# Pooled attention and a two-layer FFN on one core: the products with v in two rows of five and four key tiles per half of the queries instead of three rows of three, and p in a ring of tiles by key tile

## The chip, the cores and the metric

The kernel runs on one core of one Trainium2 chip. The metric is the device time of one launch in microseconds (us). TensorE (PE) multiplies, VectorE (DVE), ScalarE (ACT) and GpSimd (POOL) work elementwise, SyncE (SP) issues the DMAs. ns are nanoseconds.

## The reference

For 8 batches and 8 heads there are 1152 positions of 64 numbers. Pairs of neighbouring queries are averaged, so 576 queries attend to 1152 keys; the heads' results are put side by side to 4608 tokens of 512 numbers, which go through an FFN with 2048 hidden numbers.

```python
q_pool = q.reshape(B, H, S // factor, factor, D).mean(axis=3)
scores = scale * np.matmul(q_pool, k.transpose(0, 1, 3, 2))
scores = scores - np.max(scores, axis=-1, keepdims=True)
attn = np.exp(scores)
attn = attn / (np.sum(attn, axis=-1, keepdims=True) + 1e-09)
return np.matmul(attn, v).astype(np.float32)
...
h = x @ w_in
g = h - np.tanh(h)
return (g @ w_out).astype(np.float32)
```

## The kernel before

**Two stages.** The attention stage runs to about 995 us. It writes the unnormalized products with v to `x_dram` and the sums of the exponentials to `z_dram`. The FFN stage loads x back by chunks of tokens, multiplies it by the reciprocals of the sums (POOL, lines 118 to 120) and runs two layers of matmuls (`hidden`, line 521, and `second`, line 546).

**Pairs and units.** Attention goes over 32 pairs: a batch and two heads, whose 64 numbers each share the 128 partitions. A pair is cut into 36 units (`U = 4 * KT`, line 154): two halves of the 576 queries (288 each), in each half nine key tiles of 128 keys (KT is 9), in each key tile two heads. In this text units are counted from 0 to 35 within a pair, and units 36 on are the next pair's. One unit is a call of `score_unit` (line 277): two matmuls add up 128 keys x 288 queries in a tile of `ps_s` (three buffers in PSUM), and ACT writes the exponential to p. The tiles `t` that these matmuls read are `t_0_...` and `t_1_...` for even and odd pairs.

**Rows of products with v.** `pv` (line 298) multiplies p by v and adds up in `ps_o` (one buffer). Three key tiles and both heads make a group of six products; each product is two matmul instructions in the trace, so a row shows as x12. A head takes 64 of PE's columns, the two heads stand side by side (`tile_position`). The row of a group comes six units after the group's last exponential: units 5, 11, 17, 23, 29 and 35 of a pair, after that unit's scores.

**Sums.** For each group POOL adds its three p tiles into a tile `z` (`z_part`, line 292). Behind the first row of the next half, `z_sums` (line 318) adds these up over the keys with six products of 32 columns into a tile of `ps_s`; ACT copies the result (`z_out`, line 334) and SP stores it. `o_out` (line 328) copies `ps_o` after a half's last row.

**What else runs in the same units.** The maxima of the next pair's scores: 14 parts (`max_part`, line 237) of two matmuls each (the last has one) into `ps_m` (two buffers), at units 12, 14, 16, 19, 21, 23, 26, 28, 30, 33, 35, 37, 40 and 42, each followed by a reduction on DVE (the tile `mx`). The copies and differences of the next keys and queries: ACT at units 26, 28 and 30 (`x<-kq`), DVE at 34, 36 and 38 (`kq_l`). The FFN's weights: every 34 units one block (`w_block`, line 367) with five operations on DVE, 17 to 27 units into the block, two on ACT and two on POOL. At the end of the stage SP and POOL bring the first chunk of x (`x0`, lines 417 to 421), one quarter at a time.

**What sets the order.** All engines' instructions of this stage are kept in the order in which the code makes them (`InOrder`, line 27; in the trace most have its line, L37). Work is put down for a unit with `add(u, ...)`; a unit runs the list `first`, then its scores, then the list `at`, and then the row that falls on it (lines 475 to 498). In the FFN stage the order is made by the framework's scheduler.

**Tiles of p.** `pf` holds four tiles of a group, 128 x 2 heads x 3 key tiles x 288; `zp` holds four tiles `z`.

Of the kernel before, what the change touches and what calls it, by code (L numbers as in the profile page):

```python
# [8 lines left out]
F32 = mybir.dt.float32  # L9
# [3 lines left out]
ALU = mybir.AluOpType  # L13
# [30 lines left out]
def kernel(  # L44
# [18 lines left out]
    P = 128  # L63
# [3 lines left out]
    KT = S // P  # L67
# [64 lines left out]
    t, n = chunks.pop()  # L132
# [4 lines left out]
    with ExitStack() as actx:  # L137
# [1 line left out]
        wp = actx.enter_context(tc.tile_pool(name="wp", bufs=1))  # L139
        sm = actx.enter_context(tc.tile_pool(name="sm", bufs=2))  # L140
        op = actx.enter_context(tc.tile_pool(name="op", bufs=1))
        pf = actx.enter_context(tc.tile_pool(name="pf", bufs=4))
        zp = actx.enter_context(tc.tile_pool(name="zp", bufs=4))
        vp = actx.enter_context(tc.tile_pool(name="vp", bufs=2))
        ld = actx.enter_context(tc.tile_pool(name="ld", bufs=2))
        ps_m = actx.enter_context(tc.tile_pool(name="ps_m", bufs=2, space=PSUM))
# [2 lines left out]
        pe, act, dve, pool, sp = (InOrder(tc, e) for e in (nc.tensor, nc.scalar, nc.vector, nc.gpsimd, nc.sync))  # L149

        HQ = SQ // 2
        CH = S // 3
        n_pair = B * NP
        U = 4 * KT
        G = 6

# [25 lines left out]
        pairs = {}  # L182
# [94 lines left out]
        def score_unit(w, half, h, kt, p):  # L277

            ks = slice(SQ + kt * P, SQ + (kt + 1) * P)
            qs = slice(half * HQ, (half + 1) * HQ)  # L280
            ps = ps_s.tile([P, 512], F32, name="ps_s")
            x1, x2 = t1[w.i][:, h], t2[w.i][:, h]
            pe.matmul(ps[:, 0:HQ], x1[:, ks], x1[:, qs], start=True, stop=False)
            pe.matmul(ps[:, 0:HQ], x2[:, ks], x2[:, qs], start=False, stop=True)
            act.activation(p, ps[:, 0:HQ], AF.Exp, scale=1.0 / 16)

        class Group:
            pass

        late = []  # L290

        def z_part(grp):

            z = grp.z = zp.tile([P, 2, HQ], F32, name="z")
            pool.tensor_tensor(z, grp.p[:, :, 0], grp.p[:, :, 1], op=ALU.add)
            pool.tensor_tensor(z, z, grp.p[:, :, 2], op=ALU.add)

        def pv(u, grp):

            w, hf = grp.w, grp.half  # L300
            if grp.g == 0:
                hf.o = ps_o.tile([P, 512], F32, name="ps_o")
                hf.zs = []
            for j in range(3):
                kt = 3 * grp.g + j
                for h in range(2):
                    pe.matmul(hf.o[64 * h:64 * h + 64, 0:HQ], w.v[:, h, kt], grp.p[:, h, j], start=(kt == 0),
                              stop=(kt == KT - 1), tile_position=(0, 64 * h))
            hf.zs.append(grp.z)
            if grp.g == 2:  # L310
                add(u + 1, o_out, w, hf, at=first)
                late.append((w, hf))
                if w is pairs.get(n_pair - 1) and hf.n == 1:
                    add(u + G, lambda: z_sums(u + G, *late.pop()))
            elif late:
                z_sums(u, *late.pop())

        def z_sums(u, w, hf):

            ps = ps_s.tile([P, 512], F32, name="ps_s")  # L320
            for g in range(3):
                for h in range(2):
                    r = 64 * (g % 2) + 32 * h
                    pe.matmul(ps[r:r + 32, 0:HQ], ones, hf.zs[g][:, h], start=(g < 2), stop=(g > 0),
                              tile_position=(0, r))
            add(u + 1, z_out, u + 1, w, hf, ps, at=first)
# [85 lines left out]
        for i, blk in enumerate(blocks):  # L412
            u = U // 2 + 34 * i
# [19 lines left out]
        for pi in range(n_pair):  # L433
            u = pi * U
# [31 lines left out]
        def run(u, at=at):  # L466

            while at.get(u):
                at[u].pop(0)()

        for u in range(min(at), 0):
            run(u, first)
            run(u)
        groups = []
        for u in range(end + 60):
            run(u, first)
            if u < end:
                pi, r = divmod(u, U)
                half, r = divmod(r, U // 2)
                g, r = divmod(r, G)  # L480
                h, j = divmod(r, 3)
                if r == 0:
                    grp = Group()
                    if g == 0:
                        grp.half = Group()
                        grp.half.n = half
                    else:
                        grp.half = groups[-1].half
                    grp.w, grp.g = pairs[pi], g
                    grp.p = pf.tile([P, 2, 3, HQ], F32, name="p_f")  # L490
                    groups.append(grp)
                score_unit(grp.w, half, h, 3 * g + j, grp.p[:, h, j])
                if r == G - 1:
                    add(u + 1, z_part, grp)
            run(u)
            n, slot = divmod(u - 2 * G + 1, G)
            if slot == 0 and 0 <= n < len(groups):
                pv(u, groups[n])
        assert not any(at.values())


# [15 lines left out]
    def hidden(x_h, x_l, n, fc):  # L517
        h = ps_h.tile([P, 512], F32, name="ps_h")[:, 0:n]
        mm = [(w, x, c) for w, x in ((0, x_h), (0, x_l), (1, x_h)) for c in range(NP)]
        for j, (w, x, c) in enumerate(mm):  # L520
            nc.tensor.matmul(h, wi[fc][:, w, c], x[:, c, 0:n], start=(j == 0), stop=(j == len(mm) - 1))  # L521

        def t(name, dtype=F32, bufs=2):
            return gp.tile([P, 512], dtype, name=name, bufs=bufs)[:, 0:n]
        u, th, s1, s2, w, m = t("g_u"), t("g_t"), t("g_s1"), t("g_s2"), t("g_w"), t("g_m", bufs=1)
        g_h, g_l = t("g_hi", F32R, LAG + 1), t("g_lo", F32R, LAG + 1)
        nc.scalar.activation(u, h, AF.Square)  # L527
        nc.scalar.activation(th, h, AF.Tanh)
        nc.scalar.activation(s2, u, AF.Square, bias=pc[:, 1:2])  # L529
        nc.scalar.activation(s1, u, AF.Square, bias=pc[:, 0:1])  # L530
        nc.scalar.activation(m, u, AF.Relu, bias=pc[:, 2:3])
        nc.vector.scalar_tensor_tensor(w, u, -P0, h, op0=ALU.add, op1=ALU.mult)  # L532
        nc.vector.tensor_tensor(th, h, th, op=ALU.subtract)  # L533
# [89 lines left out]
```

## Time and profile before

| what | us |
|---|---|
| median of 3 runs | 1829.13 |
| lowest and highest run | 1827.97 and 1831.86 |
| the profiled execution's own time | 1830.94 |
| its span, first to last instruction | 1829.2 |
| PE busy | 1742.4 |
| DVE busy | 1384.6 |
| ACT busy | 1082.5 |
| POOL busy | 1063.9 |

The span is 1.7 us shorter than the time of the same execution. Busy time of PE is the union of its matmuls, which overlap; how long a piece of its work keeps it is read from one start to the next. "PEld" are its weight loads. A line of a timeline gives start, duration and count of instructions of one kind in sequence, and in brackets how long the engine was idle before them and what ended that. A line of the waits gives who waited for whom, the sum in us, the number of waits and the longest.

### The profile page before, as it was taken

What the parts mean: (1) busy time and instruction counts of PE and PEld (TensorE: products, weight loads), DVE (VectorE), ACT (ScalarE), POOL (GpSimd) and SP (SyncE); (2) the same over time, 40 slices, a digit from 0 to 9 for tenths busy, and PEclk for the clock granted to TensorE, in tenths of its full rate; (3) what the DMA queues carried; (4) which work ended last, traced back from release to release, by engine and by line L of the source; (5) the groups of instructions that cost most, each with busy time, mean ns of one, the idle gap of its engine ahead of it and who ended that gap; (6) DMA issues with size and microseconds to landing.
All of it is one profiled execution on the core that took longest, in us unless ns stands there. A gap on an engine that the chain in (4) does not pass through costs nothing. (4 is left out here: it accounts for less than half of the span.)

```text
span 1829.2 us, 28257 instructions
## 1 busy us (share of the span) xinstructions
PE 1742.4 (95%) x9920; PEld 1308.2 (72%) x9920; DVE 1384.6 (76%) x1815; ACT 1082.5 (59%) x2469; POOL 1063.9 (58%) x768
## 2 busy tenths in 40 slices
PE   4999999999999989999997999999999999999998
PEld 3666666766676666666664767878787888888886
DVE  5876668677667777786740788888889899988897
ACT  2555555656565555555653656666666666666676
POOL 2676678777787767777876375352535344433432
PEclk9999999999999999999998999999999999999999
DMA  7777687878878686878764822020201020101000
GB/s 208 204 181 208 175 220 204 222 199 220 224 209 233 168 213 180 214 210 229 194 167 129 312 54 68 5 66 6 64 7 64 7 63 15 47 12 35 26 18 18
DMA packets 104141, 242.28 MB, mean 132 GB/s; under 512 B 18113, under 2 KB 43329, under 8 KB 104001
## 3 DMA queue, kind: packets, MB, share of 16 engines
q1 hardware_dynamic: 104000, 240.49, 47.8%
q8 instruction: 78, 1.28, 0.3%
q14 instruction: 63, 0.51, 0.1%
HBM read 109.64 MB, written 36.42 MB: 80 GB/s over the span
## 5 line engine op out<-in xcount | busy, mean ns | idle before, releaser
L37 DVE TENSOR_REDUCE mx<-ps_m 128x2 f32<-128x768 f32 x448 | 405.8, 924 | 264.1 <-PE ps_m L37 263.8
L37 ACT ACTIVATE p_f<-ps_s 128x288 f32<-128x288 f32 x1152 | 418.1, 412 | 190.2 <-PE ps_s L37 165.4
L37 PE MATMUL ps_s<-t 128*128 128x288 f32 (+1 forms) x2304 | 447.9, 314 | 14.9 <-ACT p_f L37 8.8
L37 PEld LDWEIGHTS ps_s<-t 128*128 128x128 f32 (+1 forms) x2304 | 357.6, 191 | 119.5 <-issue 90.4
L539 POOL TENSOR_TENSOR g_lo<-g_s,g_hi 128x512 fp32r<-128x512 f32 (+1 forms) x160 | 210.2, 1315 | 394.5 <-ACT g_hi L538 338.7
L37 POOL TENSOR_TENSOR z<-p_f 128x576 f32<-128x576 f32 x192 | 287.7, 1498 | 156.2 <-PE ps_s L37 110.8
L521 PE MATMUL ps_h<-x,wi 128*128 128x512 f32 (+1 forms) x1440 | 326.9, 371 | 0.0
L37 PE MATMUL ps_o<-p_f,v 128*64 128x288 f32 x2304 | 326.0, 419 | 0.0
L37 POOL TENSOR_TENSOR z<-z,p_f 128x576 f32<-128x576 f32 x192 | 290.8, 1515 | 17.7 <-ACT p_f L37 3.0
L521 PEld LDWEIGHTS ps_h<-x,wi 128*128 128x128 f32 x1440 | 255.9, 189 | 52.1
L546 PE MATMUL ps_o<-wo,g_hi 128*128 128x512 f32 x1008 | 274.9, 392 | 3.5 <-ACT g_hi L538 3.4
L37 PE MATMUL ps_m<-x,bd 128*128 128x384 f32 x864 | 238.5, 356 | 32.1 <-DVE mx L37 17.3
L37 PEld LDWEIGHTS ps_o<-p_f,v 128*64 128x64 f32 x2304 | 150.0, 138 | 114.9 <-issue 30.1
L546 PEld LDWEIGHTS ps_o<-wo,g_hi 128*128 128x128 f32 x1008 | 186.8, 188 | 45.5 <-ACT g_hi L538 6.5
L532 DVE SCALAR_TENSOR_TENSOR g_w<-g_u,ps_h 128x512 f32<-128x512 f32 (+1 forms) x160 | 100.4, 628 | 111.6 <-PE ps_h L521 68.8
L527 ACT ACTIVATE g_u<-ps_h 128x512 f32<-128x512 f32 (+1 forms) x160 | 87.8, 549 | 158.2 <-PE ps_h L521 158.1
L37 PEld LDWEIGHTS ps_m<-x,bd 128*128 128x128 f32 x864 | 143.8, 196 | 49.7 <-DVE mx L37 27.1
L546 PE MATMUL ps_o<-wo,g_lo 128*128 128x512 f32 x504 | 159.5, 393 | 6.5 <-POOL g_lo L539 6.3
L538 ACT ACTIVATE g_hi<-g_s 128x512 fp32r<-128x512 f32 (+1 forms) x160 | 94.3, 589 | 119.4 <-DVE g_s L537 117.3
L534 DVE SCALAR_TENSOR_TENSOR g_w<-g_w,g_u 128x512 f32<-128x512 f32 (+1 forms) x160 | 164.6, 1029 | 0.0
L537 DVE COPY_PREDICATED g_s<-g_m,g_t 128x512 f32<-128x512 int32 (+1 forms) x160 | 134.4, 840 | 14.6 <-DVE g_s L536 0.5
L536 DVE SCALAR_TENSOR_TENSOR g_s<-g_s,g_w 128x512 f32<-128x512 f32 (+1 forms) x160 | 126.8, 792 | 17.1 <-DVE g_w L535 0.5
(60 smaller groups left out, 1913.3 us busy)
## 6 DMA issues: line engine op xcount, KB each, us to landing
t<-x SPq DMA_DIRECT2D x64, 432.0 KB
q_n<-in_q_dram SPq DMA_DIRECT2D x32, 576.0 KB
kq<-in_k_dram SPq DMA_DIRECT2D x32, 576.0 KB
t<-kq_l SPq DMA_DIRECT2D x64, 288.0 KB
t<-x SPq DMA_DIRECT2D x64, 288.0 KB
v<-in_v_dram SPq DMA_DIRECT2D x32, 576.0 KB
bd<-x SPq DMA_DIRECT2D x64, 144.0 KB
t<-kq_l SPq DMA_DIRECT2D x64, 144.0 KB
```

The costliest lines, as they stand in the source:

```text
L37: ins = self.tc.keep_in_program_order(f(*args, **kwargs))
L521: nc.tensor.matmul(h, wi[fc][:, w, c], x[:, c, 0:n], start=(j == 0), stop=(j == len(mm) - 1))
L527: nc.scalar.activation(u, h, AF.Square)
L532: nc.vector.scalar_tensor_tensor(w, u, -P0, h, op0=ALU.add, op1=ALU.mult)
L534: nc.vector.scalar_tensor_tensor(w, w, PL, u, op0=ALU.mult, op1=ALU.mult)
L536: nc.vector.scalar_tensor_tensor(s1, s1, P1, w, op0=ALU.add, op1=ALU.mult)
L537: last = nc.vector.copy_predicated(s1, m.bitcast(I32), th).ins
L538: nc.scalar.activation(g_h, s1, AF.Copy)
L539: nc.gpsimd.tensor_tensor(g_l, s1, g_h.bitcast(F32), op=ALU.subtract)
L546: nc.tensor.matmul(po[j], g[:, ts], wo[fc][:, w], start=(fc == 0 and i == 0), stop=(fc == NF - 1 and i == 2))
```

## The change

A half's nine key tiles are multiplied by v in two rows, key tiles 0 to 4 and 5 to 8, each four units after the last exponential it needs: units 13, 21, 31 and 39 of a pair in place of 5, 11, 17, 23, 29 and 35. `z_sums` stays behind a half's first row, so it moves from units 11 and 29 to 13 and 31, and its store and what follows it by two units. `o_out` comes after units 21 and 39. The two heads of a key tile now follow each other; before, a group did three key tiles of one head and then of the other. p is a ring of twelve tiles of 128 x 2 heads x 288, one for each key tile, as much memory as before; `zp` has five tiles in place of four. Neither the number of products nor that of POOL's additions changes.

```diff
-        pf = actx.enter_context(tc.tile_pool(name="pf", bufs=4))
-        zp = actx.enter_context(tc.tile_pool(name="zp", bufs=4))
+        pf = actx.enter_context(tc.tile_pool(name="pf", bufs=12))
+        zp = actx.enter_context(tc.tile_pool(name="zp", bufs=5))
...
-        G = 6
+        blocks_v = ((0, 5), (5, 9))
...
+        def z_part(hf, g):
+
+            z = zp.tile([P, 2, HQ], F32, name="z")
+            hf.zs.append(z)
+            pool.tensor_tensor(z, hf.p[3 * g], hf.p[3 * g + 1], op=ALU.add)
+            pool.tensor_tensor(z, z, hf.p[3 * g + 2], op=ALU.add)
+
+        def pv(u, hf, k0, k1):
+
+            w = hf.w
+            if k0 == 0:
                 hf.o = ps_o.tile([P, 512], F32, name="ps_o")
-                hf.zs = []
-            for j in range(3):
-                kt = 3 * grp.g + j
+            for kt in range(k0, k1):
                 for h in range(2):
-                    pe.matmul(hf.o[64 * h:64 * h + 64, 0:HQ], w.v[:, h, kt], grp.p[:, h, j], start=(kt == 0),
+                    pe.matmul(hf.o[64 * h:64 * h + 64, 0:HQ], w.v[:, h, kt], hf.p[kt][:, h], start=(kt == 0),
                               stop=(kt == KT - 1), tile_position=(0, 64 * h))
-            hf.zs.append(grp.z)
-            if grp.g == 2:
+            if k1 == KT:
                 add(u + 1, o_out, w, hf, at=first)
                 late.append((w, hf))
                 if w is pairs.get(n_pair - 1) and hf.n == 1:
-                    add(u + G, lambda: z_sums(u + G, *late.pop()))
+                    add(u + 6, lambda: z_sums(u + 6, *late.pop()))
             elif late:
                 z_sums(u, *late.pop())
...
+        then = {}
         for u in range(end + 60):
             run(u, first)
             if u < end:
                 pi, r = divmod(u, U)
                 half, r = divmod(r, U // 2)
+                kt, h = divmod(r, 2)
                 if r == 0:
+                    hf = Half()
+                    hf.w, hf.n, hf.p, hf.zs = pairs[pi], half, [], []
+                if h == 0:
+                    hf.p.append(pf.tile([P, 2, HQ], F32, name="p_f"))
+                score_unit(hf.w, half, h, kt, hf.p[kt][:, h])
+                if h == 1 and kt % 3 == 2:
+                    add(u + 1, z_part, hf, kt // 3)
+                for k0, k1 in blocks_v:
+                    if h == 1 and kt == k1 - 1:
+                        add(u + 4, pv, u + 4, hf, k0, k1, at=then)
             run(u)
-            n, slot = divmod(u - 2 * G + 1, G)
-            if slot == 0 and 0 <= n < len(groups):
-                pv(u, groups[n])
+            run(u, then)
```

**PE around unit 29** of pair 12, before: from the second half's part of unit 28 on. `ps_m` are the parts of the maxima, `ps_o` a row with v, `ps_s<-z,ones` the sums, `ps_s<-t` scores. The count is of products.

```order
L37 MATMUL ps_m<-x,bd_125 128x384 x2
L37 MATMUL ps_s<-t_0_121 128x288
L37 MATMUL ps_s<-t_0_122 128x288
L37 MATMUL ps_o<-p_f,v 64x288 x6
L37 MATMUL ps_s<-z,ones 32x288 x6
L37 MATMUL ps_s<-t_0_121 128x288
L37 MATMUL ps_s<-t_0_122 128x288
L37 MATMUL ps_m<-x,bd_125 128x384 x2
L37 MATMUL ps_s<-t_0_121 128x288
L37 MATMUL ps_s<-t_0_122 128x288
```

PE at the same place of the same pair now, again from the part of unit 28 on:

```order
L37 MATMUL ps_m<-x,bd_125 128x384 x2
L37 MATMUL ps_s<-t_0_121 128x288
L37 MATMUL ps_s<-t_0_122 128x288
L37 MATMUL ps_s<-t_0_121 128x288
L37 MATMUL ps_s<-t_0_122 128x288
L37 MATMUL ps_m<-x,bd_125 128x384 x2
L37 MATMUL ps_s<-t_0_121 128x288
L37 MATMUL ps_s<-t_0_122 128x288
L37 MATMUL ps_o<-p_f,v 64x288 x10
L37 MATMUL ps_s<-z,ones 32x288 x6
```

The part of unit 30 used to come behind a row and the sums; now it stands ahead of the row of ten, which comes after unit 31.

**PE around the change of pairs** (units 39 to 42 of pair 12, that is 3 to 6 of pair 13), before: from the scores of unit 39 on.

```order
L37 MATMUL ps_s<-t_1_123 128x288
L37 MATMUL ps_s<-t_1_124 128x288
L37 MATMUL ps_s<-t_1_123 128x288
L37 MATMUL ps_s<-t_1_124 128x288
L37 MATMUL ps_m<-x,bd_125 128x384 x2
L37 MATMUL ps_s<-t_1_123 128x288
L37 MATMUL ps_s<-t_1_124 128x288
L37 MATMUL ps_o<-p_f,v 64x288 x6
L37 MATMUL ps_s<-t_1_123 128x288
L37 MATMUL ps_s<-t_1_124 128x288
L37 MATMUL ps_m<-x,bd_125 128x384
```

PE from the scores of unit 39 on now:

```order
L37 MATMUL ps_s<-t_1_123 128x288
L37 MATMUL ps_s<-t_1_124 128x288
L37 MATMUL ps_o<-p_f,v 64x288 x8
L37 MATMUL ps_s<-t_1_123 128x288
L37 MATMUL ps_s<-t_1_124 128x288
L37 MATMUL ps_m<-x,bd_125 128x384 x2
L37 MATMUL ps_s<-t_1_123 128x288
L37 MATMUL ps_s<-t_1_124 128x288
L37 MATMUL ps_s<-t_1_123 128x288
L37 MATMUL ps_s<-t_1_124 128x288
L37 MATMUL ps_m<-x,bd_125 128x384
```

The row stood between the part of unit 4 (the pair's 13th, x2) and that of unit 6 (the last, one product); now a row of eight stands ahead of both.

**ACT from unit 22 to 32** of pair 12, before: from the copy of `ps_o` on. `p_f` are exponentials, `x<-kq` the copies of keys and queries, `w_hl` belongs to a weight block, `z_s` is the copy of the sums.

```order
L37 ACTIVATE o_s<-ps_o 128x288
L37 ACTIVATE p_f<-ps_s 128x288 x3
L37 ACTIVATE x<-kq 128x576
L37 ACTIVATE p_f<-ps_s 128x288 x2
L37 ACTIVATE x<-kq 128x576
L37 ACTIVATE w_hl<-w_4431 128x512
L37 ACTIVATE p_f<-ps_s 128x288
L37 ACTIVATE z_s<-ps_s 128x288
L37 ACTIVATE p_f<-ps_s 128x288
L37 ACTIVATE x<-kq 128x576
```

ACT at the same place now, from the copy of `ps_o` on:

```order
L37 ACTIVATE o_s<-ps_o 128x288
L37 ACTIVATE p_f<-ps_s 128x288 x5
L37 ACTIVATE x<-kq 128x576
L37 ACTIVATE p_f<-ps_s 128x288 x2
L37 ACTIVATE x<-kq 128x576
L37 ACTIVATE w_hl<-w_4577 128x512
L37 ACTIVATE p_f<-ps_s 128x288 x2
L37 ACTIVATE x<-kq 128x576
L37 ACTIVATE p_f<-ps_s 128x288
L37 ACTIVATE z_s<-ps_s 128x288
```

The copies of keys and queries keep their units, but the copy of `ps_o` comes two units earlier and that of the sums two units later.

More of the change, by code (lines that the diff above doesn't have):

```diff
@@ L285, in score_unit @@
             act.activation(p, ps[:, 0:HQ], AF.Exp, scale=1.0 / 16)
-        class Group:
+        class Half:
             pass
         late = []
[L292 to L301, printed above, removed]
+        def z_part(hf, g):
[6 more added lines that the diff above has]
+            if k0 == 0:
                 hf.o = ps_o.tile([P, 512], F32, name="ps_o")
-                hf.zs = []
-            for j in range(3):
-                kt = 3 * grp.g + j
+            for kt in range(k0, k1):
                 for h in range(2):
-                    pe.matmul(hf.o[64 * h:64 * h + 64, 0:HQ], w.v[:, h, kt], grp.p[:, h, j], start=(kt == 0),
+                    pe.matmul(hf.o[64 * h:64 * h + 64, 0:HQ], w.v[:, h, kt], hf.p[kt][:, h], start=(kt == 0),
                               stop=(kt == KT - 1), tile_position=(0, 64 * h))
-            hf.zs.append(grp.z)
-            if grp.g == 2:
+            if k1 == KT:
                 add(u + 1, o_out, w, hf, at=first)
@@ L473 @@
             run(u)
-        groups = []
+        then = {}
         for u in range(end + 60):
@@ L479 @@
                 half, r = divmod(r, U // 2)
-                g, r = divmod(r, G)
-                h, j = divmod(r, 3)
+                kt, h = divmod(r, 2)
                 if r == 0:
[L483 to L494, printed above, removed]
+                    hf = Half()
[8 more added lines that the diff above has]
+                        add(u + 4, pv, u + 4, hf, k0, k1, at=then)
             run(u)
-            n, slot = divmod(u - 2 * G + 1, G)
-            if slot == 0 and 0 <= n < len(groups):
-                pv(u, groups[n])
+            run(u, then)
         assert not any(at.values())
```

## The prediction

> **The bound.** I read the page first, then the waits of the attention stage (60 to 960 us), then TensorE's timeline there.
>
> ```profile
> span 1829.2 us, 28257 instructions
> PE 1742.4 (95%) x9920; PEld 1308.2 (72%) x9920; DVE 1384.6 (76%) x1815; ACT 1082.5 (59%) x2469; POOL 1063.9 (58%) x768
> ```
>
> PE at 95% could still be PE waiting inside long matmuls, so the waits decide: who waits for whom in the stage that the change touches (us, times, longest).
>
> ```profile
> DVE mx L37 <- PE ps_m L37: 247.1, 162, 4.0
> POOL z L37 <- PE ps_s L37: 107.7, 50, 5.1
> PE ps_m L37 <- DVE mx L37: 20.8, 21, 1.9
> PEld ps_s L37 <- ACT p_f L37: 18.4, 51, 1.1
> PE ps_s L37 <- ACT p_f L37: 5.1, 15, 0.6
> PEld ps_s L37 <- POOL z L37: 3.5, 8, 0.4
> ```
>
> VectorE and Pool wait for PE by the hundred us; PE waits for VectorE's maxima 20.8 us and for ScalarE's exponentials 5.1 us (some of the 18.4 us of its weight loads beside that). So PE sets the pace through attention, and time taken off PE's own stream comes off the stage, as long as nobody new falls behind.
>
> **A row** costs something beyond its products. PE's timeline, one row of three key tiles and what stands around it (start, us, count):
>
> ```profile
> 504.09 0.80 PE L37 MATMUL ps_s<-t 128*128 128x288 f32 x4
> 504.72 0.51 PE L37 MATMUL ps_m<-x,bd 128*128 128x384 f32 x2
> 505.07 0.70 PE L37 MATMUL ps_s<-t 128*128 128x288 f32 x4
> 505.61 0.52 PE L37 MATMUL ps_m<-x,bd 128*128 128x384 f32 x2
> 505.96 0.70 PE L37 MATMUL ps_s<-t 128*128 128x288 f32 x4
> 506.50 0.51 PE L37 MATMUL ps_m<-x,bd 128*128 128x384 f32 x2
> 506.94 1.68 PE L37 MATMUL ps_o<-p_f,v 128*64 128x288 f32 x12
> 508.55 1.08 PE L37 MATMUL ps_s<-t 128*128 128x288 f32 x6
> ```
>
> and the one place where two rows stand together, at the end of the stage:
>
> ```profile
> 986.76 3.13 PE L37 MATMUL ps_o<-p_f,v 128*64 128x288 f32 x24
> 989.83 0.69 PE L37 MATMUL ps_s<-z,ones 128*32 128x288 f32 x8
> ```
>
> Since matmuls overlap, I count from start to start. Two maximum matmuls take 505.96 - 505.61 = 0.35 us before scores but 506.94 - 506.50 = 0.44 before a row: 0.09 to enter. Four score matmuls take 505.61 - 505.07 = 0.54 us, but 504.72 - 504.09 = 0.63 just behind a row: 0.09 to get going again. The row itself takes 508.55 - 506.94 = 1.61 us for 12 instructions; the one place where two rows stand together takes 3.07 for 24, so 12 instructions alone are 3.07 - 1.61 = 1.46 and 0.15 is the way out. One row less is worth 0.09 + 0.09 + 0.15 = 0.33 us, and its products still cost 0.122 us an instruction wherever they stand.
>
> ```profile
> L37 PE MATMUL ps_o<-p_f,v 128*64 128x288 f32 x2304 | 326.0, 419 | 0.0
> ```
>
> 2304 / 12 = 192 rows become 128 (each product is two instructions, so a row of five tiles is 20 of them, of four 16). One of the 64 that go was the merged row at 986.76, which paid no entrance of its own. 63 x 0.33 = -20.8 us.
>
> **The transition.** PE's last products are not what the FFN waits for; this chain is, on ScalarE, the DMA queue and PE:
>
> ```profile
> 971.50 0.41 ACT L37 ACTIVATE z_s<-ps_s 128x288 f32<-128x288 f32 x1 [2.30 <-PE ps_s L37]
> 971.94 0.55 SPq L37 DMA_DIRECT2D z_dram<-z_s  x1
> 973.97 0.42 SPq L37 DMA_DIRECT2D x_f<-x_dram  x1
> 1007.33 2.93 PE L521 MATMUL ps_h<-x,t 128*128 128x512 f32 x6 [5.78 <-POOL x L37]
> ```
>
> The copy of half 61's z lets SyncE go on to the first x load, and four load-and-normalize turns later, 33 us, PE has its x. That z is summed behind the first row of half 62: before at unit 1127 and after a row of three tiles, now at unit 1129 and after a row of five. Two units cost 0.36 us each there (six in 964.91 - 962.75 = 2.16), two more tiles 8 x 0.122 = 0.98: +1.7 us.
>
> ```profile
> 962.75 2.23 PE L37 MATMUL ps_s<-t 128*128 128x288 f32 x12
> 964.91 1.68 PE L37 MATMUL ps_o<-p_f,v 128*64 128x288 f32 x12
> ```
>
> **New waits.** While PE is in a row it feeds neither VectorE nor ScalarE, and both catch up. Stretches of six units become stretches of ten and eight, and PE may outrun them. VectorE's work per part, and the five operations of a weight block (one block of each 34 units, spread over ten units):
>
> ```profile
> L37 DVE TENSOR_REDUCE mx<-ps_m 128x2 f32<-128x768 f32 x389 | 364.5, 953 | 238.1 <-PE ps_m L37 237.9
> L37 DVE TENSOR_SCALAR w<-w 128x512 int32<-128x512 int32 x64 | 50.5, 790 | 0.1
> L37 DVE SCALAR_TENSOR_TENSOR w<-w,w 128x512 int32<-128x512 int32 x32 | 36.3, 1135 | 0.2
> L37 DVE SCALAR_TENSOR_TENSOR w<-w_raw,w 128x512 f32<-128x512 uint16 x32 | 28.6, 893 | 0.2
> L37 DVE TENSOR_SCALAR w<-w 128x512 f32<-128x512 f32 x32 | 22.8, 712 | 1.2 <-ACT w L37 1.2
> ```
>
> and when reductions start (the parts begin at 504.72, above):
>
> ```profile
> 505.27 2.73 DVE L37 TENSOR_REDUCE mx<-ps_m 128x2 f32<-128x768 f32 x3 [1.02 <-PE ps_m L37]
> ```
>
> Take units 22 to 31. PE needs 10 x 0.27 + 4 x 0.35 + 0.1 = 4.2 us; VectorE four reductions, 3.8 us, so without a block it keeps up. The fourth part (unit 30) may start 3.6 us into the stretch and needs the buffer of the second (unit 26). With a block in its worst place two of its operations (0.79 + 1.14) precede that reduction, whose predecessor (unit 23, its part at 0.64) can start only about 1.2 us in, since a reduction follows its part's start by 505.27 - 504.72 = 0.55: 1.2 + 2 x 0.95 + 1.93 = 5.0, so PE waits 1.4 us. The block moves two units a pair, so 18 placements recur; the neighbours of the worst give 0.65, 0.4, 0.35, 0.35 and 0.2, the others nothing: 3.4 us per 18 pairs, 6 for the kernel. The parts at units 6 and 12 lose a row ahead of them in the same way; I take 8 us for both. Against it, the present waits stand mostly at the part of unit 4 (the one of 1.39 us at 197.81, quoted below, comes behind the scores of units 2 to 4), which now has a row of four tiles ahead of it in place of one of three (0.49 us longer) and loses up to 21 x 0.49 = 10 us of them. Bounds: -10 (only the relief) and +33 (every one of the 32 blocks costs about one more wait of the mean length, 20.8 / 21 = 1.0 us). I take 6 + 8 - 10 = +4 us, near the waits' own row, since a wait today is 1.0 us and the new ones must first use up the lead that VectorE's 247.1 us of waiting shows.
>
> For ScalarE, its two operations, and where its exponentials stand to the scores (these begin at 962.75, above):
>
> ```profile
> L37 ACT ACTIVATE p_f<-ps_s 128x288 f32<-128x288 f32 x1086 | 394.6, 412 | 176.7 <-PE ps_s L37 152.7 <-PE ps_m L37 0.4
> L37 ACT ACTIVATE x<-kq 128x576 fp32r<-128x576 f32 x87 | 60.3, 693 | 0.4 <-POOL kq L37 0.4
> ```
>
> ```profile
> 963.38 2.05 ACT L37 ACTIVATE p_f<-ps_s 128x288 f32<-128x288 f32 x6 [1.72 <-PE ps_s L37]
> ```
>
> The three copies of a pair's keys and queries (units 26, 28, 30) now fall into one stretch, where two did before and the third into the next. An exponential starts 963.38 - 962.75 = 0.63 us behind the start of its scores; queued ones start (2.05 - 0.41) / 5 = 0.33 us apart, and a copy, with the same overlap of 0.08, puts 0.61 between. Unit 26's scores begin 1.53 us into the stretch, so unit 27's exponential, behind a copy, ends at 1.53 + 0.63 + 0.33 + 0.61 + 0.41 = 3.51; unit 30's scores need its slot and could begin at 3.30. That is 0.2 us x 30 pairs = +6. The stretch that held the third copy loses about as much, -6. With the weight blocks' own two copies I take +2 us, bounds -6 and +15 (both copies of all 32 blocks costing 0.23 more).
>
> **Elsewhere.** A fifth z tile ends Pool's waits for the sums (107.7 us), but PE's weight loads wait 3.5 us for z in all: 0, at best -3. The exponentials wait for no p tile now; the ring still holds 12 tiles and each is read by both readers 11 units or more before it is written again: 0. A dozen FFN instructions of the first token chunk trade places: 0, give or take 2.
>
> The clock: these rows show a wait of 1.39 us for VectorE, a row of 12 that then takes 2.79 us in place of 1.68, and around it 40 us with the granted clock (third number from the end) at 0.96, which is 1.6 us lost.
>
> ```profile
> 195.44 0.97 PE L37 MATMUL ps_s<-t 128*128 128x288 f32 x6
> 197.81 0.88 PE L37 MATMUL ps_m<-x,bd 128*128 128x384 f32 x2 [1.39 <-DVE mx L37]
> 199.10 2.79 PE L37 MATMUL ps_o<-p_f,v 128*64 128x288 f32 x12
> ```
>
> ```profile
> 180.00:220.00 40.00, 38.43 (x252) 27.22 (x252) 25.92 (x35) 22.74 (x62) 27.95 (x20) 0.96 0.71 195
> ```
>
> So a wait can cost a slow spell on top of itself. With a few such spells among the 21 waits, six us more of waiting bring about half a spell: +1 us, bounds -5 and +5. The Trainium skill (TensorE: Matmul & The Clock Gate, section "Why this matters for your kernels") has it that PE-idle gaps of more than about 3 us between bursts bring the clock down. By that rule no wait of this stage (1.9 us at most) would slow the clock, the term would be 0 and the time a microsecond less; the row at 197.81 speaks against the rule.
>
> **Sum.** -20.8 + 1.7 + 4 + 2 + 1 = -12.1 us: span 1829.2 to 1817.1. The profiled execution took 1830.94 us, so 1818.8; the median of the three runs is 1829.13, 1.8 us less, and from there I predict 1817 us.
>
> **Rivals.**
>
> Rival 1. VectorE takes over in the long stretches (slower). Mechanism: a stretch of ten units with a whole weight block gives VectorE 3.8 + 4.3 = 8.1 us of work while PE needs 4.2, and two buffers of maxima give 1.9 us of lead: PE is 2.0 us short. If, of each of the 32 blocks, half of that is paid, that is 1.0 us more a block, the +33 above: 1829.1 - 20.8 + 1.7 + 33 + 2 + 1 = 1846; even is 17 us, so it decides from about 0.5 us of new waits a block. For it: 20.8 us of such waits exist already in stretches of six, and each may bring a slow spell. Against it: VectorE itself waits 247.1 us, and a stretch of ten is followed by a row of 2.6 us.
>
> Rival 2. The gain is eaten (same). Waits of about 17 to 20 us in all, from VectorE and ScalarE together: about 1829. PE then shows fewer us in rows and as many more in waits.
>
> Rival 3. The row ahead of unit 4 clears the present waits and the new ones stay inside the lead: -20.8 + 1.7 - 10 = 1800.
>
> Rival 4. The change doesn't do what it says: what I call entrance and exit belongs to the products, and ten products cost 5/3 of a row (1.61 x 5/3 = 2.68). Then 0.15 a half is not saved, only 0.18: 63 x 0.18 = 11 us, which with the other terms gives 1826 at most. Only one merged row in the trace speaks against it.
>
> **The numbers.** What the measurement can tell from no change is about 0.2%, 3.7 us. The forecast, 1804 to 1825.4: 0.60. Rival 3, below 1804: 0.07. Rivals 2 and 4, 1825.5 to 1832.8: 0.10 and 0.03. Rival 1, above: 0.20, of which I leave half outside. So faster 0.67, same 0.13, slower 0.20; leaving out 0.07 below and about 0.10 above, the range is 1804 to 1838.
>
> **The test.** Right: PE rows of x20 and x16 that take about 2.6 and 2.1 us start to start; score matmuls behind them as before; PE's waits for mx between 15 and 35 us, at units 6, 12 and 30 more than at 4; Pool's waits for the sums mostly gone; the FFN's main work starting near 994 us in place of 1007. Wrong: PE waits for mx of 40 us or more, or PE's weight loads waiting for exponentials twice as long; more stretches with a clock of 0.96; or a second stage whose length differs from 822 us (1829.2 - 1007.3) by more than 2.

## The result, and the profile after

The changed kernel takes **1876.55 us** (median of 5 runs, 1873.23 to 1883.38) against 1829.13 us: 1.0253 of the time before, 95% interval 1.0239 to 1.0267. The forecast was 1817 us, so not only the size but the sign was wrong. The profiled execution took 1875.1 us, 44.2 us more than that of before. Of the runs further down, three in a slower state are left out of all times (two of the four of e7_hold_14, 2707 and 3351 us, and one of e3_after_no_w, 3329).

The page begins like this (span, then busy time, share and instructions of each engine):

```profile
span 1873.3 us, 28547 instructions
PE 1748.8 (93%) x9920; PEld 1328.0 (71%) x9920; DVE 1420.8 (76%) x1815; ACT 1084.7 (58%) x2469; POOL 1059.8 (57%) x768
```

As many instructions as before on every engine; PE is busy for 6.4 us more, VectorE for 36.2 us more, and PE's share fell from 95% to 93%. The waits of the attention stage (60 to 960 us; us, times, longest), to be set beside those of before:

```profile
DVE mx L37 <- PE ps_m L37: 242.8, 164, 5.7
POOL z L37 <- ACT p_f L37: 141.8, 91, 7.2
PEld ps_s L37 <- ACT p_f L37: 37.3, 67, 4.0
PE ps_m L37 <- DVE mx L37: 30.7, 45, 2.9
PE ps_s L37 <- ACT p_f L37: 22.4, 23, 3.7
ACT w L37 <- DMA w_raw<-in_moe_w_in_dram: 7.9, 2, 4.5
ACT x L37 <- POOL kq L37: 6.4, 5, 2.7
ACT w L37 <- DMA w_raw<-in_moe_w_out_dram: 2.8, 1, 2.8
```

Pool no longer waits for the sums, as forecast. PE waits 30.7 us for maxima in place of 20.8, and **22.4 us for exponentials in place of 5.1**, once for 3.7 us. ScalarE in turn waits for the raw weights of a block.

PE's rows themselves are what the forecast said (PE's timeline):

```profile
502.69 2.65 PE L37 MATMUL ps_o<-p_f,v 128*64 128x288 f32 x20
505.27 1.16 PE L37 MATMUL ps_s<-z,ones 128*32 128x288 f32 x12
...
509.77 2.16 PE L37 MATMUL ps_o<-p_f,v 128*64 128x288 f32 x16
511.87 0.54 PE L37 MATMUL ps_s<-t 128*128 128x288 f32 x2
```

From start to start a row of twenty takes 2.58 us and one of sixteen 2.10, so eight matmul instructions more than in a row of twelve (1.61) cost 0.97, 0.121 each (a product is two of them).

Where the time went, from unit 36 to unit 1116 (pairs 1 to 30), added up from the trace's rows of PE and of its granted clock:

| pairs 1 to 30 | before | after | difference |
|---|---|---|---|
| length, us | 892.6 | 931.9 | +39.3 |
| PE idle, us | 29.7 | 60.9 | +31.2 |
| PE at half clock, us | 13.6 | 58.0 | +44.4, half of it lost: +22.2 |
| the rest | 856.1 | 842.0 | -14.1 |

The half clock is granted in windows of 3.41 us: 4 of them before, 17 after (three of the 14 spells are two windows long). After, 2.9 us of the idle time lie inside such windows and are counted in both rows, so the 22.2 is up to 1.5 us too large, and the last row's drop as much too large. Of the 44.1 us that the span grew, 39.3 lie here, 1.3 from there to the FFN's main work, which begins 40.6 us late,

```profile
1047.94 4.38 PE L514 MATMUL ps_h<-x,t 128*128 128x512 f32 x11 [5.54 <-POOL x L37]
```

and 3.5 in the rest of the FFN stage (825.4 us in place of 821.9).

**One block of weights in both kernels** shows what happened. Before (one fence from the timelines of SyncE, ScalarE and PE): the load of the raw weights is issued behind the ten copies that build the next operands; ScalarE comes to the copy that needs it and waits 3.01 us, with the exponentials behind it in its queue.

```profile
292.79 0.68 SPq L37 DMA_DIRECT2D w_raw<-in_moe_w_in_dram  x1
...
299.76 0.66 ACT L37 ACTIVATE w<-w_raw 128x512 f32<-128x512 f32 x1 [3.01 <-DMA w_raw<-in_moe_w_in_dram]
...
298.48 1.68 PE L37 MATMUL ps_o<-p_f,v 128*64 128x288 f32 x12
300.78 0.97 PE L37 MATMUL ps_s<-t 128*128 128x288 f32 x4 [0.62 <-ACT p_f L37]
```

PE meanwhile has three score buffers to fill and then its row at 298.48: of 3.01 us it loses 0.62. The same block after:

```profile
305.14 0.70 SPq L37 DMA_DIRECT2D w_raw<-in_moe_w_in_dram  x1
...
312.29 0.66 ACT L37 ACTIVATE w<-w_raw 128x512 f32<-128x512 f32 x1 [4.49 <-DMA w_raw<-in_moe_w_in_dram]
...
309.15 0.42 PE L37 MATMUL ps_s<-t 128*128 128x288 f32 x2
313.31 1.33 PE L37 MATMUL ps_s<-t 128*128 128x288 f32 x4 [3.73 <-ACT p_f L37]
314.43 0.84 PE L37 MATMUL ps_m<-x,bd 128*128 128x384 f32 x2
```

The load lands some 7 us after its issue in both (292.79 to 299.76, 305.14 to 312.29), but no row stands within the next units: PE fills its buffers and loses 3.73 us, and then its four score matmuls take 314.43 - 313.31 = 1.12 us in place of 0.54, because the clock is halved. It stays so to 317.5, another 2.1 us lost: one block cost 0.62 us before and about 6 after.

ScalarE's hold-ups of 0.5 us and more by loads and by Pool (60 to 960 us) agree. The four by raw weights before (7.6 us in all) cost PE 0.6 us ahead of its scores, the three after (10.7 us) 8.7. After, five waits of its copies for Pool's keys and queries (6.4 us, all at unit 29) cost PE 7.1, and four waits of 0.65 to 1.06 us that fall beside a row (units 13 and 31) cost it nothing.

### The profile page after: what moved, and what is told of

Same layout as the page of the kernel before. It is cut to its first block, busy times and chain, and to the rows that moved or that the text cites. A ratio compares the mean times of both kernels' runs of the same rounds, so it can differ in the third digit from the quotient of the medians.

```text
span 1873.3 us, 28547 instructions
## 1 busy us (share of the span) xinstructions
PE 1748.8 (93%) x9920; PEld 1328.0 (71%) x9920; DVE 1420.8 (76%) x1815; ACT 1084.7 (58%) x2469; POOL 1059.8 (57%) x768
## 5 line engine op out<-in xcount | busy, mean ns | idle before, releaser
L37 PEld LDWEIGHTS ps_s<-t 128*128 128x128 f32 (+1 forms) x2304 | 365.3, 193 | 114.0 <-issue 64.0
L37 PE MATMUL ps_m<-x,bd 128*128 128x384 f32 x864 | 244.8, 364 | 51.5 <-DVE mx L37 33.9
L37 PEld LDWEIGHTS ps_o<-p_f,v 128*64 128x64 f32 x2304 | 160.3, 142 | 122.8 <-issue 39.5
L539 PE MATMUL ps_o<-wo,g_lo 128*128 128x512 f32 x504 | 159.4, 392 | 10.6 <-POOL g_lo L532 10.6
L37 ACT ACTIVATE z_s<-ps_s 128x288 f32<-128x288 f32 x64 | 26.3, 411 | 201.1 <-PE ps_s L37 201.1
```

The costliest lines, as they stand in the source:

```text
L37: ins = self.tc.keep_in_program_order(f(*args, **kwargs))
L539: nc.tensor.matmul(po[j], g[:, ts], wo[fc][:, w], start=(fc == 0 and i == 0), stop=(fc == NF - 1 and i == 2))
```

## The experiments

**Theory A (cover).** ScalarE and VectorE are held up now and then in both kernels: by a load, by Pool, by a long piece of their own work. PE runs on for as long as its buffers last: three score tiles for ScalarE, two tiles of maxima for VectorE. If a row begins by then, it covers the rest. With rows at units 5, 11, 17 and so on, a row stands at one of the next three units, or at the same one, at 24 of a pair's 36 units; with rows at 3, 13, 21 and 31 at 16. What is no longer covered idles PE, and the halved clock adds to it. **Rivals:** the loads simply come too late (B); VectorE is the new bound (C, the forecast's rival 1); or the ring of p tiles and the order of the heads cost the time.

**e1_three_rows:** all of the change but the grouping and place of the rows.

```diff
-        blocks_v = ((0, 5), (5, 9))
+        blocks_v = ((0, 3), (3, 6), (6, 9))
...
-                        add(u + 4, pv, u + 4, hf, k0, k1, at=then)
+                        add(u + 6, pv, u + 6, hf, k0, k1, at=then)
```

> The new tiles of p, the new order of heads and the fifth z tile, but three rows of three key tiles at their old places (six units after a row's last exponential). If the rows covered VectorE and ScalarE, and nothing else in the change costs anything: 1829 us give or take 4, PE's waits for mx about 22 us as before. If the tiles or the order of heads cost the time: 1870 or more.

Measured: 1825.1 us, 0.9963 of before (0.9948 to 0.9977). The ring, the fifth z tile and the order of the heads cost nothing and gain a little; the loss belongs to the two rows, their size and their place.

**e2_hi_in_row:** ScalarE's three copies of a pair (units 26, 28 and 30) all behind the exponential of unit 31, where a row stands.

```diff
+            if pi > 2:
+                units.update(hi_q=-77, hi_k=-77)
...
-                add(u + units[what + "_k"] + step, f, pi, 2 * SQ, KQ)
+                add(u + units[what + "_k"] + (0 if pi > 2 and what == "hi" else step), f, pi, 2 * SQ, KQ)
```

> The changed kernel with the three copies of keys and queries put down for unit 31 together, so that ScalarE does them while PE is in the row of ten. If the long stretch overloads ScalarE: the waits at unit 30 (11 us) go, and with them some slow spells of the clock, so 1876 falls to 1855 to 1865. If VectorE is all of it: 1876 stays within 4.

Measured: 1867.0 us, 1.0186 (1.0148 to 1.0224), between the two times that were expected. Added up by unit over pairs 2 to 30, PE's idle time ahead of the scores of unit 30 fell from 9.1 to 0.3 us, that ahead of its maxima rose from 4.2 to 8.8. By the medians these copies' place is worth a fifth of the loss.

**e3_after_no_w and e4_before_no_w:** the kernel after and the kernel before, each with VectorE's five operations of a block replaced by two memsets (these kernels leave out the FFN's weights).

```diff
-                          (17, lambda: ts(whole(t[0]), whole(t[0]), -top, top, op0=ALU.max, op1=ALU.min)),
...
-                          (27, lambda: stt(whole(t[2]), lo, 2.0 ** -36, whole(t[2]), op0=ALU.mult, op1=ALU.mult)),
+                          (17, lambda: dve.memset(t[1], 0)),
+                          (27, lambda: dve.memset(t[2], 0)),
```

> The changed kernel without VectorE's five operations per weight block (two fills in their place; the FFN's weights are left out that way). If VectorE's bursts make the new waits: PE's waits for mx fall from 34 to under 10 us, the clock's slow spells mostly go, and the time is 1825 to 1840. If ScalarE makes them: above 1855.

> The kernel before with the same left out, as control (the FFN's weights are left out). Its waits for mx (22 us) go: 1805 to 1820 us. If VectorE's bursts are the whole reason for the loss, e3 is then 15 to 20 us below this run, which is the gain of the rows left out; if ScalarE is as much of it, e3 stays above it.

Measured: 1857.95 us after (1.0133, 1.0107 to 1.016) and 1800.51 before (0.9831, 0.9815 to 0.9847), the latter below what was expected. Taking the same work off VectorE gained 30.3 us before and 18.6 after: the change loses 57 us *without* that work. C in its plain form falls. In e3_after_no_w PE waits 12.4 us for maxima and 30.0 for exponentials: what VectorE no longer holds up meets the next hold-up, on ScalarE.

**e5_loads_early and e9_before_loads:** the loads of a block 10 units earlier and of queries and keys 8 units earlier, in the kernel after and in the kernel before.

```diff
-            add(u, w_block, u, *blk)
+            add(u - 10, w_block, u, *blk)
...
-            units = dict(load=-98, query_sums=-86, hi_q=-82, hi_k=-80, max_queries=-76, lo_q=-74, lo_k=-72, operands=-35, load_v=-30)
+            units = dict(load=-106, query_sums=-86, hi_q=-82, hi_k=-80, max_queries=-76, lo_q=-74, lo_k=-72, operands=-35, load_v=-30)
```

> The changed kernel with two loads issued earlier and nothing else moved: the raw weights of a block 10 units ahead of where they were, the queries and keys of a pair 8 units ahead. Theory A (cover): ScalarE is held up at points where its next operation waits for a DMA or for Pool; a hold-up reaches TensorE only if no row stands within the next three units, and two rows a half leave more units without one. Taking away the causes that come from late loads (ScalarE waits 10.7 us for w_raw and 6.4 us for kq between 60 and 960 us) takes away a part of it: TensorE's waits for exponentials fall from 26.7 to about 12 us, five to eight half-clock spells go, 1850 to 1865 us. Theory B (the loads alone): the stretches run so fast that the data come late, and that is all: at most 1832 us. Theory C (VectorE sets the loss): TensorE's waits for maxima stay at 34 us and the time stays within 0.3% of 1876.

> The kernel before with the same two loads issued earlier as in e5_loads_early. Theory A: there ScalarE waits 7.6 us for w_raw and 0.4 us for kq and TensorE 5.1 us for exponentials, since a row stands within the next three units at 24 of 36 units, so early loads are worth 0 to 6 us: 1823 to 1830 us, against the 30 us that they gave in the changed kernel. If early loads are worth 20 us or more here too (1810 or less), the late loads have nothing to do with the change.

Measured: 1845.8 us after (1.0076, 1.0048 to 1.0104), 30.7 less and more than A gave; 1826.3 before (0.9974, 0.9961 to 0.9987), 4.7 less. PE's waits of e5_loads_early (60 to 960 us):

```profile
PE ps_m L37 <- DVE mx L37: 32.4, 45, 2.9
...
PE ps_s L37 <- ACT p_f L37: 4.8, 15, 0.5
```

The waits for exponentials are back where they were before the change (4.8 against 5.1 us), and the half clock fell from 58.0 to 34.1 us. So late loads made ScalarE's share of the loss, and they cost the kernel before almost nothing, as A says; B alone would have brought all of it back (at most 1832). The waits for maxima have not moved.

**e6_lag6:** rows six units behind their last key tile in place of four, at units 5, 15, 23 and 33.

```diff
-                        add(u + 4, pv, u + 4, hf, k0, k1, at=then)
+                        add(u + 6, pv, u + 6, hf, k0, k1, at=then)
```

> The changed kernel with its rows six units behind their last key tile in place of four (rows at units 5, 15, 23 and 33 of a pair in place of 3, 13, 21 and 31). The stretches are as long as before the move, so Theory A (too few places with a row near) gives 1860 to 1890 us; if the rows only stand in an unlucky place against the fixed positions of the copies and reductions, the time moves by more than 20 us, to 1850 or less if the new place is a better one.

Measured: 1898.7 us (1.0362, 1.0328 to 1.0395), above what A gave. As many units are covered, but others: the transpose of the row maxima at unit 15 has lost the row at 13 ahead of it, and PE waits there for 35.7 us in all (pairs 2 to 30). The count of covered units isn't enough; it matters which work stands at the open ones.

**e7_hold_14 and e8_hold_19:** the same hold-up at two places. Four copies more on ScalarE in each of 29 pairs, behind the exponential of unit 14, seven units ahead of a row, or of unit 19, two ahead of it.

```diff
+        idle = op.tile([P, 576], F32, name="idle")
+        nc.gpsimd.memset(idle, 1.0)
+
+        def blocked():
+            for _ in range(4):
+                act.activation(idle, idle, AF.Copy)
...
+            if 2 <= pi < 31:
+                add(u + 14, blocked)
```

> The changed kernel with four more copies on ScalarE (128x576 on a tile that nobody else uses, about 2.5 us together) once a pair, behind the exponential of unit 14, in pairs 2 to 30: just behind a row, seven units ahead of the next. TensorE has three score buffers, so it can run through units 15, 16 and 17 (about 1.3 us) and then stands: Theory A gives about 2.0 us of waiting in each of 29 pairs, and, if a standstill of this size also brings one window of 3.4 us at half clock, 1.7 us more: 29 x 2.0 = 58 without and 29 x 3.7 = 107 with it, so 1935 or 1985 us. If only the sum of ScalarE's work mattered (it idles some 370 us in this stage), nothing or the same as in the run with the copies behind unit 19.

> The same four copies behind the exponential of unit 19, two units ahead of the row at unit 21. TensorE runs through units 20 and 21 and then through the row of sixteen (2.1 us) while ScalarE is held up: Theory A gives about 0 to 0.8 us a pair and no half-clock spell of its own, 1876 to 1900 us. If the place does not matter, the same as the copies behind unit 14.

Measured: at unit 14 the profiled execution took 1935.3 us, 60.2 more than that of the changed kernel, and one other run 1945.2; at unit 19 the median is **1877.8 us** (1.0255, 1.0227 to 1.0283) against 1876.55. Timelines of ScalarE and PE with the copies at unit 14:

```profile
479.48 2.82 ACT L37 ACTIVATE idle<-idle 128x576 f32<-128x576 f32 x4
...
482.65 0.98 PE L37 MATMUL ps_s<-t 128*128 128x288 f32 x4 [1.29 <-ACT p_f L37]
```

and at unit 19:

```profile
468.43 2.83 ACT L37 ACTIVATE idle<-idle 128x576 f32<-128x576 f32 x4
...
469.18 2.16 PE L37 MATMUL ps_o<-p_f,v 128*64 128x288 f32 x16
471.27 0.88 PE L37 MATMUL ps_s<-t 128*128 128x288 f32 x4
```

The same 2.8 us stop PE for 1.29 in the open stretch, and not at all where it is in a row meanwhile: the place of a hold-up decides, not its length. The price at unit 14 was mis-sized, and that 1935 us was one of the two expected times is luck: it stood for 58 us of waiting and no half clock. PE was idle 28.8 us more in pairs 1 to 30 (89.7 against 60.9) and spent 51.2 us more at half clock (109.2 against 58.0), of which half, 25.6, is lost: 54.4 us together, of a stretch that grew by 59.4.

**e10_three_loads:** e1_three_rows with the loads of e5_loads_early.

> Three rows of three with the ring by key tile (e1_three_rows) and the loads earlier. Theory A: little, as for the kernel before: 1815 to 1825 us. If the loads are worth 20 us or more whatever the rows, 1805 or less.

Measured: 1815.9 us (0.9925, 0.9909 to 0.9941), 9 us less than e1_three_rows: early loads help three rows a little, and two rows much.

**e11_lo_in_rows and e12_all_in_rows:** the changed kernel with early loads and fixed work put at rows; the second one puts the operations of a block there as well.

```diff
-            row, steps = -26, (5, 8, 14)
+            row, steps = -23, (2, 5, 11)
...
+            lo_at = (-77, -69, -59)
...
+                if what == "lo" and pi > 2:
+                    for x, c in zip(lo_at, (0, SQ, 2 * SQ)):
+                        add(u + x, f, pi, c, c + SQ)
+                    continue
```

```diff
+            rows = [x for x in range(u + 10, u + 80) if x % 18 in (3, 13)]
-            for i, op in ((12, begin),
+            for i, op in ((rows[0], begin),
...
-                add(u + i, op)
+                add(i, op)
```

> The changed kernel with the loads earlier, and VectorE's work of fixed position put at rows: the three subtractions that make the low parts at units 31, 3 and 13 in place of 34, 0 and 2, the row maxima at unit 13 in place of 10 (their transpose stays at 15). Theory A holds for VectorE too (its cover is two buffers of maxima): the waits at the part of unit 6 (19.3 us in e5_loads_early) and at unit 16 (10.3 us) mostly go, TensorE waits for maxima fall from 32 to 8 to 15 us, and about seven half-clock spells go with them: 1845.8 - 20 - 12 = 1814, 1805 to 1825 us, so faster than the kernel before. If VectorE is short of time as a whole, the waits move to other units and the time stays above 1835.

> As e11_lo_in_rows, and the seven operations of a weight block on ScalarE and VectorE put at rows too (one or two a row, so a block takes about 44 units from its first operation to its store in place of 28). Theory A: the waits of TensorE for VectorE and ScalarE in attention fall to some 10 us in all and hardly a half-clock spell is left: 1795 to 1812 us. If VectorE's work collects behind the rows, its next reductions are late and the waits for maxima grow over those of e11_lo_in_rows: 1820 or more.

Measured: 1800.4 us (0.9839, 0.9819 to 0.9859) and **1791.2 us (0.9784, 0.9767 to 0.9802)**, both faster than the kernel before, and by more than A gave. PE's waits in e12_all_in_rows:

```profile
PE ps_m L37 <- DVE mx L37: 5.5, 7, 1.5
...
PE ps_s L37 <- ACT p_f L37: 3.7, 4, 1.6
```

In pairs 1 to 30 PE is at half clock for 6.8 us in place of 58.0 (in e11_lo_in_rows never). In e11_lo_in_rows PE's idle time ahead of the part of unit 6 is gone (18.0 us in e5_loads_early, pairs 2 to 30). VectorE wasn't short of time: it is busy for 1424.9 us here, no less than in the kernel after.

**e13_three_all_in_rows and e14_after_again:** the moves of e12_all_in_rows given to three rows of three, at units 5, 11, 17, 23, 29 and 35; and the changed kernel once more beside it.

> Three rows of three (at units 5, 11, 17, 23, 29 and 35 of a pair) with the same early loads and the same work put at rows as in e12_all_in_rows: subtractions at 29, 35 and 5, row maxima at 11, a block's operations at the rows from its tenth unit on. Between this kernel and e12_all_in_rows only the grouping of the products differs, with TensorE's waits small in both. Theory A: the row term of the forecast is right (63 x 0.33 = 20.8 us less 1.7 at the transition), so this one takes 1791 + 19 = 1810 us, 1804 to 1816. If putting work at rows is what made e12_all_in_rows fast and the grouping is worth nothing, 1791 us; if a product costs the same in any row (rival 4 of the forecast), 1798 to 1802.

> The changed kernel once more, beside the one with three rows: 1870 to 1885 us, to have both ends of the comparison on one chip.

Measured: 1826.3 us (0.9983, 0.9972 to 0.9995), 10 above the range that A gave, and 1869.8 us (1.0215, 1.0191 to 1.0239). So the moved work doesn't help three rows: they take 10 us more than in e10_three_loads. Their waits:

```profile
PE ps_m L37 <- DVE mx L37: 26.0, 30, 1.4
```

Moves that fit rows of 2.1 and 2.6 us may not fit rows of 1.6, but that isn't shown, and there is a rival: VectorE is busy for 1479.6 us here, with as many operations as in e10_three_loads (1405.3) and e12_all_in_rows (1424.9). A block's five operations take 187.4 us in all in place of 139.9 and 147.1, the three subtractions 130.4 in place of 110.7 and 113.2; they overlap Pool's instructions for 234 us in place of 173 and 165, and the last section shows VectorE held up by Pool. No run separates the two. The 35 us between this kernel and e12_all_in_rows are therefore waits and rows together. Taking PE's idle time and half of the time at half clock off pairs 1 to 30, as in the table above, leaves 859.0 us here and 832.8 in e12_all_in_rows; for e4_before_no_w and e3_after_no_w 852.2 and 835.9, for e10_three_loads and e5_loads_early 856.0 and 843.4. With the 14.1 us of the table above these are four comparisons: two rows save 12.6 to 16.3 us by three of them and 26.2 by the one with this kernel; the forecast's 0.33 us for each of these 60 halves is 19.8.

## Why the prediction was wrong

**The bound** was read rightly: PE paces, and all that was lost was lost on PE.

**A row: right by its length.** Over all rows between 60 and 960 us that ran at full clock with no idle time before what follows, a row of twelve takes 1.606 us before (176 rows), one of sixteen 2.091 and one of twenty 2.576 after (52 and 49): 0.121 us an instruction against 0.122, and 3 x 1.606 - 2.091 - 2.576 = 0.15 us less a half for the way out, as forecast. Rival 4, with 2.68 us for a row of twenty, fails. The rest of the table shows less than the 19.8 us in three of the four comparisons (12.6 to 16.3); where the difference went isn't shown.

**The transition:** +1.3 us measured from unit 1116 to the FFN's main work, +1.7 forecast.

**New waits, VectorE: mis-sized.** By PE's idle time ahead of the parts of each unit (pairs 2 to 30), the relief at unit 4 has the size that was forecast (10.6 us became 0.8, -9.8 against -10), but by luck: 9 waits stood there, not 21, and they lost 1.1 us each, not 0.49. Unit 30 came nearly as forecast (4.2 against 6). Units 6 and 12 were put at 8 together and took 16 more: unit 6 went from 3.0 to 16.8. Its part needs the buffer that the reduction of the part of unit 1 frees; the subtractions at units 34 and 0 and, in the lines below, an operation of a block stand ahead of that reduction, and the row that used to come in between (at 5) is gone. e11_lo_in_rows, which moves these subtractions, has no wait left there. VectorE's and PE's timelines of the changed kernel:

```profile
107.38 1.65 DVE L37 TENSOR_SCALAR w<-w 128x512 int32<-128x512 int32 x1
108.94 0.95 DVE L37 TENSOR_REDUCE mx<-ps_m 128x2 f32<-128x768 f32 x1
109.81 1.60 DVE L37 TENSOR_TENSOR kq_l<-kq,x 128x576 fp32r<-128x576 f32 x1
...
109.94 0.44 PE L37 MATMUL ps_m<-x,bd 128*128 128x384 f32 x1 [0.88 <-DVE mx L37]
```

The forecast counted a block's operations at mean lengths (the one at 107.38 takes 1.65 us) and left the subtractions out. Together PE's waits for maxima grew by 9.9 us where 4 were taken; at 30.7 us they are still inside the 15 to 35 that the test called right.

**New waits, ScalarE: the step that failed.** The forecast priced ScalarE's own copies (+2, at most +15) and took it that ScalarE could start each of them. The list of waits of before, from which it was quoted, also had ScalarE waiting 7.6 us for raw weights (us, times, longest):

```profile
ACT w L37 <- DMA w_raw<-in_moe_w_in_dram: 5.8, 3, 3.0
ACT w L37 <- DMA w_raw<-in_moe_w_out_dram: 1.8, 1, 1.8
```

The forecast doesn't mention them. They cost PE almost nothing, because a row stood beside each: all four fall on unit 17, where there was one. PE's waits for exponentials grew by 17.3 us, and early loads took just these away.

**The clock: the largest error.** +1 us (bounds -5 and +5) against 13 windows more, +22 us (+21 without the idle time inside them). The mechanism was named, and tied to "about half a spell" for six us of waiting. Measured is 44.4 us more at half clock for 31.2 us more idle time: each us of idle brought 0.7 of lost clock with it. That price is not a constant: e14_after_again, the same kernel, has 60.5 us of idle time in these pairs and 68.3 us at half clock.

**Sum.** -14 by the rest of the table in place of -19.8 for its 60 halves, +1.3 at the transition in place of +1.7, +31 of waiting in place of +6, +22 of clock in place of +1, and 3.5 in the FFN stage, which the forecast put at 0. The last isn't explained: that stage takes 825 to 827 us in the runs with a slow attention stage and 821 to 824 in the others, and no run here was made for it.

**The rivals.** Rival 1 had the sign and 1846 us, but named VectorE alone; e3_after_no_w shows that it isn't that. (By its own terms it decides from 16 us of waits on, not 17.) What was missing is a rival on what the rows did for others: a row is also the time in which ScalarE and VectorE get over a hold-up. "Both catch up" stood in the forecast, and only the added work was priced, not the hold-ups that were there already.

## What to carry to other kernels

Before work is taken off the pacing engine in larger and fewer pieces, list every wait of the *other* engines, those too that cost nothing, and ask which piece of work hides each. Where such cover goes, issue the loads earlier and put the side work beside the pieces that are left: here this turned 47 us of loss into 40 us of gain (1791.2 against 1831.0 for the kernel before beside it), and the same moves gave three rows next to nothing (1826.3 against 1830.0).

## What the runs showed of the hardware

**Little idle time halves TensorE's clock.** PE's timeline of the changed kernel, and two windows of 3.41 us there (busy time by engine, then the granted clock):

```profile
606.89 0.62 PE L37 MATMUL ps_m<-x,bd 128*128 128x384 f32 x2 [1.22 <-DVE mx L37]
607.34 0.43 PE L37 MATMUL ps_s<-t 128*128 128x288 f32 x2
607.70 4.30 PE L37 MATMUL ps_o<-p_f,v 128*64 128x288 f32 x20
611.93 1.17 PE L37 MATMUL ps_s<-z,ones 128*32 128x288 f32 x12
```

```profile
604.32:607.73 3.41, 2.19 (x14) 1.57 (x12) 3.34 (x7) 1.80 (x6) 0.00 (x0) 0.99 0.91 223
607.73:611.14 3.41, 3.41 (x17) 1.72 (x18) 3.34 (x6) 0.41 (x1) 2.62 (x3) 0.51 1.00 211
```

1.22 us of idle time in one window, and the next one runs at 0.51: the row of twenty takes 4.23 us to the start of what follows it, in place of 2.58. The spells of this kernel all begin on one grid of 3.41 us, and the full-clock windows ahead of them hold 1.0 to 2.9 us of idle time. Other windows with up to 1.48 us had no spell behind them, so idle time alone doesn't settle it. In pairs 1 to 30 of all sixteen profiles (117 spells), no spell begins behind a window with less than 0.96 us of idle time, and none is missing behind a full-clock window with more than 1.58. The Trainium skill (TensorE: Matmul & The Clock Gate, section "Why this matters for your kernels") asks for no idle gaps of more than about 3 us; by these runs gaps a third as long are enough.

**VectorE waits for Pool within an instruction.** VectorE's and Pool's timelines of the changed kernel:

```profile
861.70 1.17 DVE L37 CAST m<-nm 128x10 fp32r<-128x10 f32 x1
862.90 1.32 DVE L37 TENSOR_TENSOR m<-nm,m 128x10 fp32r<-128x10 f32 x1
...
861.41 1.43 POOL L37 TENSOR_TENSOR z<-z,p_f 128x576 f32<-128x576 f32 x1
862.79 1.40 POOL L37 TENSOR_TENSOR z<-p_f 128x576 f32<-128x576 f32 x1
```

Ten numbers a partition take 1.17 and 1.32 us, and end when Pool's additions end (862.87 and 862.84, 864.22 and 864.19). The same cast with no Pool instruction beside it takes 0.174 us, and 31 of 32 had one beside them here (25 of 32 before). The reductions of 768 numbers that read PSUM show none of it (0.95 us with and without). By their mean lengths these two kinds took 19 us more than before, and a block's three TENSOR_SCALAR operations, 0.94 us on average in place of 0.76, another 17: of the 36.2 us by which VectorE's busy time grew, the others about cancel. That growth alone loses nothing: e1_three_rows has most of it (1418.8 us busy) and is no slower than before. The Trainium skill (SBUF — State Buffer, section "SBUF: two separate sides") has VectorE and Pool share a pair of ports that one of them holds for a whole instruction; the trace agrees.
